# An expert's second products follow its first ones by three steps instead of two

## Chip and metric

The kernel runs on one core of a Trainium2 chip. The metric is device microseconds per execution. The engines are named as in the profile: PE (matrix products), PEld (PE's weight loads, beside the products), DVE, ACT and POOL (elementwise work), SP (issues most DMAs). Each engine takes its own instructions strictly in order, so an instruction that waits holds everything queued behind it on that engine.

## What is computed

Three layers, one behind the other, on 3072 tokens of width 384.

```python
# 1. gated linear attention, 4 x 8 heads, 768 steps, head width 48
state = f[:, :, t, :, None] * state + einsum('bhd,bhe->bhde', k[:, :, t], v[:, :, t])
y[:, :, t] = einsum('bhd,bhde->bhe', q[:, :, t], state)
# 2. eight experts, one per token, and only for tokens with x @ w_skip > 0
h = maximum(xc[mask] @ w1[e], 0.0)                    # 384 -> 1024
y[mask] = gate_w[mask, None] * (h @ w2[e])            # 1024 -> 384
out[do_compute] = xc + y
# 3. dense gated layer, 384 -> 1536 -> 384, on all tokens
xn = x / rms * rms_g
return silu(xn @ w_gate) * (xn @ w_val) @ w_out
```

## The kernel before

The attention takes the first 175 us or so. It works on 24 tiles of 128 tokens and scatters each finished token row to a slot in DRAM: tokens of expert e to the 256 slots of that expert, tokens that skip the experts to a part of their own.

Then the eight experts run, one after the other, in `expert(e)`. Values are kept as pairs of 16-bit numbers, a high and a low part, so each product is made of three. `exT` holds the expert's 256 token rows, transposed. The 1024 hidden units are cut into KF = 8 blocks of 128, and a step m works on one block:

- `up(m)`, the first products: 9 matmuls (L1041) of 256 columns into the PSUM tile `ph`, of which there are four, taken in turn by m. Then `relu`: ACT writes the high part `hh` (L1044), and DVE, which needs `hh`, writes the low part `hl` (L1045).
- `down(m)`, the second products: for each of the two halves of 128 tokens three matmuls (L1088) of 384 columns, with `hh`, `hh` and `hl` as weights, added up over all m in the PSUM tiles `ey`.

The order of the steps is written out in the loop at the end of `expert`:

```python
for m in range(KF + LAG):
    if m < KF:
        up(m)
    if m >= LAG:
        down(m - LAG)
    yield
```

The tiles `hh` and `hl` have LAG + 2 buffers. Expert 0 is a special case: the first 96 of its rows were already multiplied ahead, so its `up` has 160 columns.

Each `yield` hands over to `run`, which takes steps of work for other parts from two queues, `run(expert(e), N2)` with N2 = (1.1, 2.2): on average 1.1 steps from the first and 2.2 from the second. These steps are placed behind the newest `relu` (`tc.issue_after` on its ACT and its DVE instruction). The first queue prepares weights: load a piece of an expert's w1 or w2 into one of four buffers `st` (L357, SP) and split it into high part (L406, ACT) and low part (L407, DVE). Before expert e starts, its weights' remaining steps are taken at once (`need`); expert e + 3 is put in the queue when expert e is done. The second queue finishes tokens (`place`, `first`, `middle`): add the expert's result to the token row (L483 DVE, L484 POOL; L481 POOL for rows without an expert), the sum of squares (L488 ACT), its root (L489, L490 POOL), the normed row in two parts `xn` (L494 ACT, L495 DVE), some small copies (L510 to L513, L533, L534), and then either a scatter to the DRAM tensor `xnd` (L514 POOL) or, for the tokens of blocks 0 and 1 of the dense layer, a transposing DMA into `xnT` (L535 SP).

The dense layer starts with `pair`, blocks 0 and 1 of 512 tokens, 12 first products each (L892, `pwg` and `pwv`), then their second products (L915). Its weights are split by `prep_in` (L199 to L203 and L450 on DVE, L449 on ACT), which is queued when the experts are done; the scheduler moves some of it up beside the last experts.

The written order is not the final one. A scheduler lays out each engine's queue from its own idea of times, and moves an instruction ahead where it believes the one before it would wait.

Of the kernel before, what the change touches and what calls it, by code (L numbers as in the profile page):

```python
# [52 lines left out]
XB = 13  # L53
OTB = 3
SPLIT = 2
LAG = 2
WARM2 = 0
WN = 128
WAT = 1.0
# [26 lines left out]
def fused_kernel(ctx, tc, q, k, v, f, w_skip, w_gate, w1, w2, g_gate, g_val, g_out, rms_g, out, dbg=None):  # L86
# [956 lines left out]
    def relu(hh, hl, ph):  # L1043
        a = nc.scalar.activation(out=hh, in_=ph, func=AF.Relu)  # L1044
        b = nc.vector.scalar_tensor_tensor(out=hl, in0=ph, scalar=0.0, in1=hh, op0=ALU.max, op1=ALU.subtract)  # L1045
        pins.append((a.ins, b.ins))
# [13 lines left out]
    def expert(e):  # L1060
# [13 lines left out]
        def up(m):  # L1074
            ph = ps.tile([128, 1, CAP - c0], F32, **bank(m % 4), name="ph")
            products(e, xT, ph, (m,), c0, CAP)
            if c0:
                hs[m] = [a[:, m, :] for a in h]
            else:
                hs[m] = [ek.tile([128, CAP], F16, tag="h" + a, name="h" + a, bufs=LAG + 2) for a in "hl"]  # L1080
            relu(hs[m][0][:, c0:CAP], hs[m][1][:, c0:CAP], ph[:, 0, :])

        def down(m):
            hh, hl = hs.pop(m)
            for t in range(CAP // 128):
                sl = slice(t * 128, (t + 1) * 128)
                for j, (a, w) in enumerate(((hh, w2h), (hh, w2l), (hl, w2h))):
                    nc.tensor.matmul(py[t], lhsT=a[:, sl], rhs=w[:, m, :], start=(m == 0 and j == 0), stop=(m == KF - 1 and j == 2))  # L1088
# [7 lines that stand above are left out]
# [131 lines left out]
```

## Time and profile before

| | us |
|---|---|
| median of three runs | 765.24 |
| lowest, highest | 763.53, 768.19 |
| the profiled execution | 761.93 |
| its span, first to last instruction | 760.2 |
| PE busy in the span | 718.8 (95%) |
| DVE busy | 446.9 (59%) |
| ACT busy | 340.0 (45%) |
| POOL busy | 197.6 (26%) |

The profiled execution took 1.7 us more than its span and 3.3 us less than the median. PE's busy time counts matmuls from start to modelled end, and neighbours overlap, so it says where PE sits idle, not how fast it is while busy; the granted clock says the latter. The shares are means over stages that differ: attention to about 175 us, experts to about 336, dense layer to the end.

### The profile page before, as it was taken

How to read it: one execution, taken by the hardware profiler on the slowest of the kernel's cores; microseconds unless marked ns; L12 is line 12 of the kernel's file. 1: busy time of each engine (PE TensorE's matmuls, PEld its weight loads, DVE VectorE, ACT ScalarE, POOL GpSimd, SP SyncE). 2: the span in 40 equal slices, each digit the busy share in tenths (PEclk: the TensorE clock that was granted, in tenths of full speed). 3: DMA queues.
4: the chain of work that ended last, by engine and by line, in shares of the span. 5: the costliest groups of instructions: out<-in, count | busy, mean ns of one | idle time of the engine just before them, and what ended most of it. 6: DMA issues, size and time to landing. Idle time of an engine off the chain costs nothing.

```text
span 760.2 us, 14086 instructions
## 1 busy us (share of the span) xinstructions
PE 718.8 (95%) x5452; PEld 442.6 (58%) x5452; DVE 446.9 (59%) x955; ACT 340.0 (45%) x773; POOL 197.6 (26%) x274
## 2 busy tenths in 40 slices
PE   8999989896999879799999999999999999999995
PEld 4788878785766556454444565445454554454443
DVE  2788767885788878999997100534443454332230
ACT  5878757643767766566554111221312231222131
POOL 5222455541365556554000021000200020001002
PEclk9999999998999998899999999999999999999998
DMA  9999978746588998855453410321521150001001
GB/s 156 180 195 200 209 181 206 230 134 195 160 271 263 272 232 256 274 141 199 125 167 123 84 42 32 94 61 65 166 83 65 61 167 0 1 1 43 1 0 47
DMA packets 172890, 102.25 MB, mean 135 GB/s; under 512 B 137720, under 2 KB 151336, under 8 KB 172816
## 3 DMA queue, kind: packets, MB, share of 16 engines
q1 hardware_dynamic: 168336, 88.60, 46.4%
q0 software_dynamic: 4480, 12.67, 4.5%
q8 instruction: 45, 0.74, 0.4%
q14 instruction: 29, 0.24, 0.1%
HBM read 78.33 MB, written 16.24 MB: 124 GB/s over the span
## 4 chain that ended last, share of the span: by engine, by line
PE 73%; DMA 8%; DVE 6%; ACT 4%; POOL 4%; issue 3%; SPq 0%; POOLq 0%; ACTq 0%; DVEq 0%
PE po L915 18%; PE pwv L892 18%; PE pwg L892 18%; DMA xnd<-xn,at 4%; PE sc L666 3%; PE py L682 3%; DMA st<-in_moe_w_dram 3%; PE py L677 2%; PE ptq L648 1%; PE ptk L648 1%; DVE w2l L407 1%; PE pm L658 1%; PE lg L698 1%; PE px L703 1%; POOL xs L783 1%
## 5 line engine op out<-in xcount | busy, mean ns | idle before, releaser
L898 DVE SCALAR_TENSOR_TENSOR hf<-pwv,sg 128x512 f32<-128x512 f32 x72 | 49.6, 691 | 147.1 <-PE pwv L892 126.1
L923 POOL DMA_INDIRECT out_dram<-ot,ids x24 | 23.7, 986 | 370.9 <-ACT ot L922 366.3
L892 PE MATMUL pwg<-xnT,wgh 128*128 128x512 f16 x432 | 105.5, 379 | 0.7 <-DMA xnT<-xn 0.7
L892 PE MATMUL pwv<-xnT,wvh 128*128 128x512 f16 x432 | 105.5, 379 | 0.0
L901 ACT CAST gh<-hf 128x512 f16<-128x512 f32 x72 | 44.4, 616 | 115.2 <-DVE hf L898 115.1
L915 PE MATMUL po<-wol,gh 128*128 128x384 f16 x288 | 93.7, 326 | 0.0
L915 PE MATMUL po<-woh,gh 128*128 128x384 f16 x288 | 93.7, 326 | 0.0
L915 PE MATMUL po<-woh,gl 128*128 128x384 f16 x288 | 93.4, 326 | 0.0
L896 ACT ACTIVATE sg<-pwg 128x512 f32<-128x512 f32 x72 | 42.6, 594 | 101.1 <-PE pwg L892 101.0
L915 PEld LDWEIGHTS <-gh 128*128 128x128 f16 x576 | 56.3, 98 | 41.8
L892 PEld LDWEIGHTS <-wvh 128*128 128x128 f16 x432 | 42.3, 98 | 50.5
L902 DVE TENSOR_TENSOR gl<-hf,gh 128x512 f16<-128x512 f32 x72 | 49.9, 696 | 35.9 <-ACT gh L901 35.9
L892 PEld LDWEIGHTS <-wgh 128*128 128x128 f16 x432 | 42.2, 98 | 47.7 <-issue 1.2
L1041 PE MATMUL ph<-exT,w1h 128*128 128x256 f16 (+1 forms) x384 | 58.2, 277 | 6.9 <-DMA exT<-xs 6.9
L892 PE MATMUL pwv<-xnT,wvl 128*128 128x512 f16 x216 | 58.9, 379 | 0.0
L892 PE MATMUL pwg<-xnT,wgl 128*128 128x512 f16 x216 | 58.9, 379 | 0.0
L1041 PEld LDWEIGHTS <-w1h 128*128 128x128 f16 x432 | 40.9, 102 | 19.2 <-DMA exT<-xs 7.0
L629 POOL TENSOR_TENSOR qs<-q,ep 128x384 f32<-128x384 f32 x24 | 28.8, 1202 | 73.3 <-ACT ep L625 58.1
L1088 PE MATMUL ey<-w2h,hh 128*128 128x384 f16 x112 | 37.9, 339 | 8.1 <-ACT hh L1044 8.1
L922 ACT ACTIVATE ot<-po 128x384 f32<-128x384 f32 x24 | 11.6, 489 | 61.4 <-PE po L915 53.1
L915 PEld LDWEIGHTS <-gl 128*128 128x128 f16 x288 | 28.2, 98 | 18.6
L1088 PE MATMUL ey<-w2h,hl 128*128 128x384 f16 x112 | 31.9, 342 | 6.7 <-DVE hl L1045 5.5
(204 smaller groups left out, 1383.3 us busy)
## 6 DMA issues: line engine op xcount, KB each, us to landing
st<-in_moe_w_dram SPq DMA_DIRECT2D x32, 768.0 KB, 5.7
st<-in_moe_w_gate_dram SPq DMA_DIRECT2D x12, 768.0 KB, 4.4
st<-in_moe_w_val_dram SPq DMA_DIRECT2D x12, 768.0 KB, 4.5
st<-in_moe_w_out_dram SPq DMA_DIRECT2D x12, 768.0 KB, 4.3
f<-in_f_logit_dram SPq DMA_DIRECT2D x24, 192.0 KB, 4.6
q<-in_q_dram SPq DMA_DIRECT2D x24, 192.0 KB, 4.2
k<-in_k_dram SPq DMA_DIRECT2D x24, 192.0 KB, 4.4
v<-in_v_dram SPq DMA_DIRECT2D x24, 192.0 KB, 4.5
```

Source lines behind the costliest of these rows:

```text
L629: scaled.append(nc.gpsimd.tensor_tensor(out=qs[:, :, 0:D], in0=ins["q"], in1=ep, op=ALU.mult).ins)
L666: nc.tensor.matmul(scs[r][:, j, :], lhsT=T["k"][64 * r:64 * r + 64, j, :], rhs=T["q"][64 * r:64 * r + 64, j, :], start=True, stop=True)
L682: nc.tensor.matmul(py[64 * r:64 * r + D, j, :], lhsT=ins["v"][:, 2 * j + r, :], rhs=A[r][:, j, :], start=False, stop=(j == HP - 1), skip_g ...
L892: nc.tensor.matmul(p, lhsT=w, rhs=x, start=(j == 0), stop=(j == len(terms) - 1))
L896: nc.scalar.activation(out=sg, in_=pg, func=AF.Silu, scale=1.0 / SG)
L898: nc.vector.scalar_tensor_tensor(out=hf, in0=pv, scalar=SH / SG, in1=sg, op0=ALU.mult, op1=ALU.mult)
L901: nc.scalar.copy(out=hh, in_=hf)
L902: gated.append(nc.vector.tensor_tensor(out=hl, in0=hf, in1=hh, op=ALU.subtract).ins)
L915: nc.tensor.matmul(po[t], lhsT=a[:, sl], rhs=w, start=(m == 0 and j == 0), stop=(m == KF2 - 1 and j == 2))
L923: sc = nc.gpsimd.indirect_dma_start(out=out, out_offset=bass.IndirectOffsetOnAxis(ap=at[:, t:t + 1].bitcast(U32), axis=0), in_=ot, in_offs ...
L1041: nc.tensor.matmul(out[:, i, :], lhsT=a, rhs=r, start=(j == 0), stop=(j == len(terms) - 1))
L1088: nc.tensor.matmul(py[t], lhsT=a[:, sl], rhs=w[:, m, :], start=(m == 0 and j == 0), stop=(m == KF - 1 and j == 2))
```

## The change

LAG becomes 3. So `down(m)` is written behind `up(m + 3)` instead of behind `up(m + 2)`, the tiles `hh` and `hl` have five buffers instead of four, and the loop of an expert has 11 turns instead of 10, so that `run` hands out 12.1 and 24.2 steps per expert instead of 11 and 22. No instruction of the computation is added or removed.

```diff
 OTB = 3
 SPLIT = 2
-LAG = 2
+LAG = 3
 WARM2 = 0
```

What this does to the queues is seen at three places. On PE, the start of expert 1's second products. `ph_3719` is the first product m = 2 of expert 1 before and `ph_3745` is m = 3 after; `hh_3676` and `hh_3678` are the high part of m = 0. Before:

```order
L1041 MATMUL ph_3719<-exT_3660,w1l_3477 128x256
L1088 LDWEIGHTS hh_3676
L1088 MATMUL ey0_3664<-w2h_3556,hh_3676 128x384
L1088 LDWEIGHTS hh_3676
L1088 MATMUL ey0_3664<-w2l_3557,hh_3676 128x384
L1088 LDWEIGHTS hl_3677
L1088 MATMUL ey0_3664<-w2h_3556,hl_3677 128x384
```

and now:

```order
L1041 MATMUL ph_3745<-exT_3662,w1l_3477 128x256
L1088 LDWEIGHTS hh_3678
L1088 MATMUL ey0_3666<-w2h_3550,hh_3678 128x384
L1088 LDWEIGHTS hh_3678
L1088 MATMUL ey0_3666<-w2l_3551,hh_3678 128x384
L1088 LDWEIGHTS hl_3679
L1088 MATMUL ey0_3666<-w2h_3550,hl_3679 128x384
```

`down(0)` starts one whole `up` later, right behind the last matmul of m = 3 instead of m = 2.

On DVE, from the last low part `hl` of expert 1 to the first of expert 2. Here `w2l` is a piece of a later expert's weights, and `x` begins the finishing of expert 1's tokens. Before:

```order
L1045 SCALAR_TENSOR_TENSOR hl<-ph,hh 128x256 x2
L407 SCALAR_TENSOR_TENSOR w2l<-st_3868,w2h 128x4x192
L149 TENSOR_REDUCE big<-w2h 128x1
L407 SCALAR_TENSOR_TENSOR w2l<-st_3868,w2h 128x4x192
L407 SCALAR_TENSOR_TENSOR w2l<-st_3906,w2h 128x4x192
L1045 SCALAR_TENSOR_TENSOR hl<-ph,hh 128x256
L483 SCALAR_TENSOR_TENSOR x_3939<-ey_3664,exr 128x384
```

and now:

```order
L1045 SCALAR_TENSOR_TENSOR hl<-ph,hh 128x256
L149 TENSOR_REDUCE big<-w2h 128x1
L407 SCALAR_TENSOR_TENSOR w2l<-st_3832,w2h 128x4x192
L407 SCALAR_TENSOR_TENSOR w2l<-st_3894,w2h 128x4x192 x2
L495 SCALAR_TENSOR_TENSOR xn<-x_3803,m_3806,xn 128x384
L1045 SCALAR_TENSOR_TENSOR hl<-ph,hh 128x256
L483 SCALAR_TENSOR_TENSOR x_3939<-ey_3666,exr 128x384
```

The first `hl` of expert 2 now stands behind three pieces of `w2l` and an `xn`, where it stood behind three pieces (the first row before holds two `hl`, the last of expert 1 and the one ahead of it).

On DVE, behind the last low part of expert 7, which is the last of all. The `xn` written from `x_5329` before and from `x_5292` now is the last row tile that block 1 of the dense layer waits for. Before:

```order
L1045 SCALAR_TENSOR_TENSOR hl<-ph,hh 128x256
L483 SCALAR_TENSOR_TENSOR x_5376<-ey_5032,exr 128x384
L533 COPY ms_x<-m_5332 128x1
L199 TENSOR_SCALAR fb<-st_5754 128x768
L513 TENSOR_SCALAR at<-exr 128x1
L511 COPY xn<-exr 128x4
L495 SCALAR_TENSOR_TENSOR xn<-x_5329,m_5332,xn 128x384
```

and now:

```order
L1045 SCALAR_TENSOR_TENSOR hl<-ph,hh 128x256
L511 COPY xn<-exr 128x4
L495 SCALAR_TENSOR_TENSOR xn<-x_5292,m_5303,xn 128x384
L199 TENSOR_SCALAR fb<-st_5754 128x768
L510 SCALAR_TENSOR_TENSOR ms_x<-exr,m_5368 128x1
L495 SCALAR_TENSOR_TENSOR xn<-x_5342,m_5346,xn 128x384
```

Five rows stood between that `hl` and that `xn`; now one does.

## Rows read from the trace of the kernel before

**Rows 1.** Busy time of each engine in five stretches of the span, in us (the stretch, its length, then PE, PEld, DVE, ACT and POOL with their instruction counts, the granted TensorE clock as a share of full speed, the DMA share and GB/s). The experts run from 181.5 to about 336.

```profile
181.50:195.00 13.50, 13.48 (x116) 10.76 (x117) 7.19 (x15) 6.87 (x15) 0.00 (x0) 0.88 0.81 231
195.00:246.00 51.00, 48.66 (x365) 34.64 (x364) 42.20 (x95) 37.46 (x85) 28.35 (x35) 1.00 0.78 242
246.00:297.00 51.00, 43.25 (x299) 29.27 (x297) 41.84 (x84) 33.83 (x79) 30.13 (x37) 0.93 0.96 252
297.00:336.40 39.40, 33.93 (x214) 21.21 (x211) 38.99 (x84) 24.52 (x63) 23.80 (x30) 0.91 0.78 240
340.00:470.00 130.00, 130.00 (x674) 65.77 (x673) 75.60 (x132) 46.50 (x97) 14.43 (x15) 1.00 0.38 111
```

**Rows 2.** The chain of work that ended last, from 176 to 340 us, in order of time (its shares by line, then some of its pieces: start, length, what).

```profile
by line: DMA xnd<-xn,at 16.5%; DMA st<-in_moe_w_dram 12.0%; issue 8.4%; DVE w2l L407 6.3%; PE ph L1041 4.1%; ACT w2h L406 3.8%; DVE hl L1045 3.6%; DVE xn L495 3.3%; DVE w1l L407 3.1%; PE ey L1088 3.0%; POOL m L489 2.8%; ACT w1h L406 2.8%; P
...
192.41 0.64 PE ph L1041 x9
...
196.00 6.21 DMA st<-in_moe_w_dram
...
273.32 9.69 DMA xnd<-xn,at
...
333.64 2.71 DMA xnT<-xn
...
336.49 2.10 PE pwg L892 x9
```

**Rows 3.** PE's instructions in order of time, those in the experts' part before which PE sat idle (start, length, instruction; in brackets the idle time just before it and what ended it).

```profile
210.45 0.34 PE L1088 MATMUL ey<-w2h,hh 128*128 128x384 f16 x1 [0.68 <-ACT hh L1044]
...
251.28 0.34 PE L1088 MATMUL ey<-w2h,hh 128*128 128x384 f16 x1 [0.88 <-ACT hh L1044]
...
253.41 0.50 PE L1088 MATMUL ey<-w2h,hl 128*128 128x384 f16 x2 [1.09 <-DVE ids L534]
...
264.90 0.34 PE L1088 MATMUL ey<-w2h,hh 128*128 128x384 f16 x1 [0.97 <-ACT hh L1044]
...
279.42 0.34 PE L1088 MATMUL ey<-w2h,hh 128*128 128x384 f16 x1 [0.93 <-ACT hh L1044]
...
284.55 0.50 PE L1088 MATMUL ey<-w2h,hh 128*128 128x384 f16 x1 [3.01 <-ACT hh L1044]
...
311.89 0.34 PE L1088 MATMUL ey<-w2h,hh 128*128 128x384 f16 x1 [0.45 <-ACT hh L1044]
...
316.37 0.82 PE L1088 MATMUL ey<-w2h,hl 128*128 128x384 f16 x2 [3.34 <-DVE hl L1045]
```

**Rows 4.** Groups of instructions by line from 195 to 336 us (line, engine, operation, tiles, shapes, count | busy us, mean ns of one | idle us of the engine before them and what ended it).

```profile
L1088 PE MATMUL ey<-w2h,hh 128*128 128x384 f16 x112 | 37.9, 339 | 8.1 <-ACT hh L1044 8.1
...
L1088 PE MATMUL ey<-w2h,hl 128*128 128x384 f16 x112 | 31.9, 342 | 6.7 <-DVE hl L1045 5.5 <-DVE ids L534 1.1
...
L407 DVE SCALAR_TENSOR_TENSOR w2l<-st,w2h 128x768 f16<-128x768 f32 x26 | 28.1, 1099 | 4.5 <-ACT w2h L406 4.4
L407 DVE SCALAR_TENSOR_TENSOR w1l<-st,w1h 128x768 f16<-128x768 f32 x24 | 27.5, 1145 | 0.4 <-ACT w1h L406 0.2
...
L495 DVE SCALAR_TENSOR_TENSOR xn<-x,m,xn 128x384 f16<-128x384 f32 x26 | 18.2, 700 | 5.9 <-ACT xn L494 5.5
```

**Rows 5.** Who waited for whom from 181.5 to 336 us, DVE first, then ACT (us in total, times, longest us).

```profile
DVE xn L495 <- ACT xn L494: 5.5, 7, 2.4
DVE w2l L407 <- ACT w2h L406: 5.2, 8, 2.0
DVE at L513 <- DMA xnd<-xn,at: 3.1, 1, 3.1
DVE hl L1045 <- ACT hh L1044: 2.2, 3, 1.4
...
ACT xn L494 <- POOL m L490: 12.5, 12, 2.9
...
ACT hh L1044 <- PE ph L1041: 4.7, 5, 2.0
```

**Rows 6.** PE's instructions in order of time where nothing holds them (one step of expert 1), the first full-speed second product after each of the two long stalls, and one DVE instruction beside the POOL instruction that it overlaps.

```profile
200.37 0.49 PE L1041 MATMUL ph<-exT,w1l 128*128 128x256 f16 x3
200.70 0.33 PE L1088 MATMUL ey<-w2h,hh 128*128 128x384 f16 x1
200.86 0.33 PE L1088 MATMUL ey<-w2l,hh 128*128 128x384 f16 x1
...
290.70 0.33 PE L1088 MATMUL ey<-w2h,hh 128*128 128x384 f16 x1
...
321.33 0.33 PE L1088 MATMUL ey<-w2h,hh 128*128 128x384 f16 x1
...
251.49 1.53 DVE L495 SCALAR_TENSOR_TENSOR xn<-x,m,xn 128x384 f16<-128x384 f32 x1
...
251.68 0.92 POOL L481 TENSOR_TENSOR x<-xr 128x384 f32<-128x384 f16 x1
```

**Rows 7.** The last piece of the dense layer's first weights that DVE splits (instructions in order of time), and, from the chain of work that ended last, the last first product of its blocks 0 and 1 and the second products behind it.

```profile
382.25 1.28 DVE L450 SCALAR_TENSOR_TENSOR wvl<-fb,gsc,wvh 128x256 f16<-128x256 f32 x3
...
422.12 1.94 PE pwv L892 x9
424.06 46.80 PE po L915 x288
```

## Prediction

> **What bounds the kernel now.** I read the busy time by stretch first [rows 1]. In the dense layer PE is busy 130.00 of 130 us, so nothing is to be won there by feeding it better. The experts' part, 181.5 to 336.4, is the only one that the change touches. Up to 246 PE is busy 48.66 of 51 us at full clock. From 246 to 297 it is 43.25 of 51 at a granted clock of 0.93, and from 297 to 336.4 it is 33.93 of 39.4 at 0.91. So PE loses time in the second half, while DVE is at 38.99 of 39.4 us at the end and at 41.84 of 51 before that.
>
> Next the chain that ended last in that part [rows 2]. PE holds 4.1% and 3.0% of its 164 us, 11.6 us in all, and that is the start, 181.5 to 193. From there to 336.49 the chain runs through DMAs (the `xnd` scatter 16.5%, weight loads 12.0%), DVE, ACT and POOL, and ends with an `xn`'s transposing DMA, landing after 2.71 us. That speaks against a gain: PE's stalls are not on that chain.
>
> Then the stalls themselves [rows 3], each before a `down`, and each ended by `hh` or `hl` (an `ids` copy next to an `hl` once). Counting products from the start, the rows are expert 1 m = 6 (0.68), expert 4 m = 0 (0.88, then 1.09 in the same `down`), expert 4 m = 6 (0.97), expert 5 m = 4 (0.93) and m = 5 (3.01), and expert 7 m = 0 (0.45, then 3.34). In all PE idles 8.1 + 6.7 = 14.8 us before the second products [rows 4]. The two long stalls cost more than their length. Second products after them last 0.50 us and more instead of 0.33 [rows 3, 6], which is the lower of the two clock levels, 1.2 instead of 2.4 GHz. Full speed is back at 290.70 and 321.33 [rows 6]. That is 6.15 and 4.96 us at half rate, or 3.1 and 2.5 us lost. The stalls of 0.97 and 1.09 were not followed by this.
>
> **What the change moves, and its price.** No instruction of the computation is added, so the sum is made of stalls. A `down(m)` is covered by what PE has queued between the last matmul of `up(m)` and the first of `down(m)`. Three first products start 0.33 us apart in sum, 0.11 each, and a second product takes 0.16 [rows 6]. Counted in the two built orders:
> - m = 3 and 4: 18 first and 12 second products before, 3.9 us; now 27 and 18, 5.9 us.
> - m = 5: 3.9 us before, now 18 and 18, 4.9 us. m = 6: 10 and 12, 3.1 us; now 9 and 18, 3.9 us. m = 7: 3.1 us; now 4 and 18, 3.4 us.
> - m = 0: 18 and 6, 2.9 us; now 27 and none, 2.9 us. Before, the scheduler had stretched this for experts 4 (25 and 6, 3.7 us) and 7 (27 and 6, 3.9 us); now they have 2.9 and 3.3. So the head of an expert gains nothing and at two experts loses.
>
> Step by step, if the helpers (ACT, DVE, POOL) deliver when they do now:
> - Middle stalls shown: 0.68 goes, 0.97 shrinks by 0.9, 0.93 goes, 3.01 shrinks by 1.0. Sum 3.5.
> - The small ones: 14.8 less the 11.35 of rows 3 leaves 3.45. Most lie where the cover grows by 0.3 to 2 us; I take three quarters, 2.6. With the line above 6.1 us saved.
> - Heads: at expert 4 the `hl` product now comes 0.33 us behind the first one, with 2.9 of cover; before it had 3.7 and, between the two waits, 0.87 of other products. Lost 1.3. At expert 7, 3.9 less 3.3 is 0.6 lost. Sum 2.0, rounded up.
> - Net on PE: 4.1 us, from 6.1 - 2.0.
>
> What of it reaches the end? DVE's only idle time that ends on `hh` is 2.2 us in three waits, and ACT's on `ph` 4.7 us in five, while ACT waits 12.5 us for POOL's `m`, and DVE 5.5 for `xn`, 5.2 for `w2h` and 3.1 for a scatter [rows 5]. Those are latencies among the helpers and stay as they are. So between 0 (the helpers' chain sets the end) and 4.1 us (PE does) I take the middle, 2.0 us, since the chain speaks for the first and PE's busy share to 246 for the second.
>
> The rest goes together. Buffers: a fifth `hh` and `hl` add no wait. PSUM: `up(m + 4)` needs the tile of m, and `down(m)` stands ahead of it, so the four tiles just suffice. The 11th turn hands out 1.1 and 2.2 more steps per expert, all behind the last `relu`. In the built order, DVE's queue between the last `hl` of an expert and the first of the next grows by one split piece at two boundaries (1.1 each [rows 4]), one `xn` at one (0.7 [rows 4]), about 1.2 at another and 1.0 at the last, some 5.1 in sum, none at two. Who waits for that is the next expert's `down(0)`. As DVE's total is unchanged, I count nothing for it in the forecast and price it below. SP keeps its sequence of weight loads, with a few neighbours swapped; a load still waits for one of four `st`. At the end, the last `xn` for `xnT` has five rows fewer ahead of it, two of them of an `xn`'s size (some 1.3 us by its mean of 0.70), but PE now has one `down` more queued ahead of that point, 6 times 0.16, 1.0 us. Neither counts. The dense layer can start earlier without running dry: its last weights are split at 382.25 + 1.28 = 383.5 and first used by the 21st of 24 `up`s, four of them (each two of 1.94) before 424.06, at 408.5 [rows 7]. That is 25 us of room.
>
> The profiled execution took 761.93, 3.3 below the median of 765.24. The sum gives 759.9 for a profiled one, and **763** for a median.
>
> **Rivals.**
> *Helpers set the end, no gain: 765.2.* Behind it stands the chain without PE [rows 2], and DVE full from 297 on [rows 1]. Against it is that DVE idles 9 us of the 51 before that. One `xn` lasted 1.53 us beside a POOL instruction of 0.92 [rows 6], where its mean is 0.70 [rows 4], so the two engines hold each other up at times.
> The Trainium skill, SBUF — State Buffer, section "SBUF: two separate sides", says that a DVE instruction with two SBUF inputs and a POOL instruction share one pair of ports under an exclusive lock. The row agrees; by that rule the helpers' time can't be squeezed by letting them overlap better, and this rival's time is what comes out.
>
> *PE is followed by the helpers: 756.1.* The 6.1 us of middle and small stalls go and the heads don't get worse, since a PE without stalls hands `ph` over earlier. The stall of 3.01 shrinks to 2.0 and the clock holds, 3.1 us more. Together 9.2 us. For it: PE's share to 246 and the 3.1 and 2.5 us paid for the clock. Against it: ACT waits little for `ph`.
> The Trainium skill, TensorE: Matmul & The Clock Gate, section "Loop structure matters more than you think", says that a loop that waits between its matmuls runs cold and a dense one stays at full clock. By that the change would earn the clock back besides the stalls, which is this rival; the rows behind the two long stalls agree, those behind the short ones show no loss.
>
> *The heads get worse: 775.* The mechanism is the first `hl` of an expert behind a denser DVE queue: 5.1 us of growth over five boundaries, plus 2.0 of lost cover, plus the clock falling at two more experts (2.8 each, the mean of 3.1 and 2.5), 12.7 us. With all of the middle savings it is 6.6, without them 12.7; I take 10. It decides once the first `hl` comes more than 3.3 us after its `up`; at expert 7 it came 8.4 after (3.9 + 0.45 + four products + 3.34).
>
> *The change does little that the scheduler had not done:* at experts 4 and 7 `up(3)` already stood ahead of much of `down(0)`. That gives the time of the first rival and is in its chance.
>
> **How the numbers follow.** The three runs spread over 4.7 us, 0.6%, so about 1%, 7.65 us, is what a measurement can tell from no change. Chances: forecast 0.45, no gain 0.28, PE followed 0.14, heads worse 0.13. The first two lie within 1%; of the third 0.12 lies beyond 757.6 and of the fourth 0.10 beyond 772.9. So faster 0.12, same 0.78, slower 0.10. The range for 8 in 10 takes in the first two with their bounds and some of each of the others: 754 to 774.
>
> **What would show it.** In the trace after, the `down`s of m = 3 to 6 should wait for almost nothing, and PE's idle time before second products should fall from 14.8 to some 10 us, most of it at m = 0 of experts 4 to 7. The chain between 193 and the first `pwg` should hold next to no PE, and that `pwg` should start 0 to 4 us earlier than 336.49. DVE should still be full at the end. I am wrong if the experts' part shortens by over 7 us, or if waits of over 3 us stand at the head of several experts with slow products behind them.

## The result and the profile after

The kernel became slower. Its median is 773.05 us (771.61 to 774.39) beside 765.83 for the kernel before on the same chip, a ratio of 1.0096 (95% interval 1.0069 to 1.0123); a second comparison gave 1.0122 (1.0102 to 1.0142). The forecast of 763 us was wrong in sign. The profiled execution took 773.05 us, with a span of 771.3.

The experts start 4.7 us later in this trace (186.2 instead of 181.5; the first experiment shows this to be chance). So the busy time by stretch, which answers to [rows 1], is taken with all borders 4.7 us later (same columns; the last stretch ends with the last second product):

```profile
186.20:199.70 13.50, 13.50 (x115) 10.79 (x116) 7.96 (x16) 7.83 (x16) 0.00 (x0) 0.87 0.88 256
199.70:250.70 51.00, 45.77 (x333) 32.87 (x332) 37.04 (x85) 33.83 (x78) 28.51 (x31) 0.93 0.79 221
250.70:301.70 51.00, 43.55 (x314) 30.58 (x311) 41.90 (x88) 35.12 (x80) 32.98 (x40) 0.97 0.91 251
301.70:346.00 44.30, 34.34 (x222) 21.93 (x223) 41.87 (x88) 26.18 (x65) 27.44 (x32) 0.92 0.78 222
```

In the first 51 us of the experts DVE had been busy 42.20 us and PE 48.66 at full clock [rows 1]; now it is 37.04 and 45.77 at a clock of 0.93, and the last second product comes 44.30 us into the last stretch where it came 36.5 us into it (at 333.5; the 39.4 us of [rows 1] reach on to a wait of the dense layer). DVE's total over the whole span hasn't changed, 447.0 us and 446.9 before. So DVE has no more to do; it waits more. Who it waited for (186 to 346 us, same columns as [rows 5]):

```profile
DVE at L513 <- DMA xnd<-xn,at: 6.0, 5, 2.3
DVE at L513 <- issue: 5.6, 1, 5.6
DVE xn L511 <- issue: 5.0, 1, 5.0
DVE xn L511 <- DMA xnd<-xn,at: 2.7, 1, 2.7
DVE hl L1045 <- ACT hh L1044: 2.1, 2, 1.5
...
DVE xn L511 <- DMA xnT<-xn: 0.9, 1, 0.9
```

And before, at the same copies, besides the 3.1 us in [rows 5] (181.5 to 336 us):

```profile
DVE xn L511 <- DMA xnT<-xn: 1.6, 2, 1.3
DVE xn L511 <- DMA xnd<-xn,at: 1.0, 2, 0.7
```

L511 and L513 are small copies of some 0.15 us: they put a row tile's tail into `xn` and its list of rows into `at`, just ahead of its scatter to `xnd`. Before them DVE idled 20.2 us, where it had idled 5.7. ACT's `xn`, which goes into the same buffers, waited 11.2 us for scatters, where it had waited 6.6. "issue" means that the profile names no releaser; what it was is seen further down.

PE's second products with more than 0.9 us of idle time before them, in order of time, which answers to [rows 3], and two of those behind the second stall:

```profile
232.64 0.34 PE L1088 MATMUL ey<-w2h,hh 128*128 128x384 f16 x1 [1.89 <-ACT hh L1044]
236.29 0.50 PE L1088 MATMUL ey<-w2h,hl 128*128 128x384 f16 x1 [3.15 <-DVE hl L1045]
236.58 0.53 PE L1088 MATMUL ey<-w2h,hh 128*128 128x384 f16 x1
236.90 0.53 PE L1088 MATMUL ey<-w2l,hh 128*128 128x384 f16 x1
256.81 0.34 PE L1088 MATMUL ey<-w2h,hl 128*128 128x384 f16 x1 [2.48 <-DVE hl L1045]
274.72 0.34 PE L1088 MATMUL ey<-w2h,hl 128*128 128x384 f16 x1 [1.37 <-DVE hl L1045]
277.06 0.34 PE L1088 MATMUL ey<-w2h,hl 128*128 128x384 f16 x1 [1.02 <-DVE hl L1045]
284.90 0.34 PE L1088 MATMUL ey<-w2h,hl 128*128 128x384 f16 x1 [1.79 <-DVE hl L1045]
302.31 0.34 PE L1088 MATMUL ey<-w2h,hl 128*128 128x384 f16 x1 [0.92 <-DVE hl L1045]
312.64 0.34 PE L1088 MATMUL ey<-w2h,hl 128*128 128x384 f16 x1 [0.99 <-DVE hl L1045]
315.73 0.50 PE L1088 MATMUL ey<-w2h,hl 128*128 128x384 f16 x2 [1.51 <-DVE hl L1045]
320.01 0.50 PE L1088 MATMUL ey<-w2h,hl 128*128 128x384 f16 x2 [1.17 <-DVE ids L534]
328.62 0.82 PE L1088 MATMUL ey<-w2h,hl 128*128 128x384 f16 x2 [5.50 <-DVE hl L1045]
```

Counting products, these are expert 2 m = 6 (twice), expert 3 m = 6, expert 4 m = 5 and 6, expert 5 m = 0, expert 6 m = 0, 5, 6 and 7, and expert 7 m = 0. Nearly all end on `hl`, DVE's part; before, most ended on ACT's `hh`.

**The place itself.** POOL, DVE, ACT and PE around the stall of 3.15, in order of time (start, length, instruction, idle time before it and what ended it):

```profile
219.92 1.07 POOL L514 DMA_INDIRECT xnd<-xn,at  x1 [5.09 <-DVE xn L495]
...
226.56 0.15 DVE L513 TENSOR_SCALAR at<-exr 128x1 int32<-128x1 f32 x1 [2.30 <-DMA xnd<-xn,at]
...
227.64 0.62 DVE L495 SCALAR_TENSOR_TENSOR xn<-x,m,xn 128x384 f16<-128x384 f32 x1
...
228.54 1.87 POOL L514 DMA_INDIRECT xnd<-xn,at  x1 [3.62 <-DVE xn L495]
...
235.61 0.15 DVE L513 TENSOR_SCALAR at<-xr 128x1 int32<-128x1 f32 x1 [5.62 <-issue]
235.63 0.61 ACT L494 ACTIVATE xn<-x,m 128x384 f16<-128x384 f32 x1 [2.55 <-DMA xnd<-xn,at]
235.82 0.42 DVE L1045 SCALAR_TENSOR_TENSOR hl<-ph,hh 128x256 f16<-128x256 f32 x1
236.15 0.61 DVE L495 SCALAR_TENSOR_TENSOR xn<-x,m,xn 128x384 f16<-128x384 f32 x1
...
237.05 1.18 POOL L514 DMA_INDIRECT xnd<-xn,at  x1 [3.83 <-DVE xn L495]
```

`xn` and `at` have two buffers each. Call the four row tiles A, B, C and D; in DVE's built order of the changed kernel the last three are `xn_3963`, `xn_4000` and `xn_4087`:

```
L513 TENSOR_SCALAR at_4030<-exr_3664 128x1
L511 COPY xn_4000<-exr_3664 128x4
...
L495 SCALAR_TENSOR_TENSOR xn_3963<-x2_3939,m2_3943,xn_3963 128x384
L1045 SCALAR_TENSOR_TENSOR hl_4048<-ph_4037,hh_4047 128x256
...
L1045 SCALAR_TENSOR_TENSOR hl_4077<-ph_4066,hh_4076 128x256
...
L513 TENSOR_SCALAR at_4092<-xr_4035 128x1
L511 COPY xn_4087<-xr_4035 128x4
...
L1045 SCALAR_TENSOR_TENSOR hl_4108<-ph_4097,hh_4107 128x256
L495 SCALAR_TENSOR_TENSOR xn_4000<-x2_3992,m2_3996,xn_4000 128x384
L495 SCALAR_TENSOR_TENSOR xn_4087<-x2_4059,m2_4062,xn_4087 128x384
```

A's scatter is issued at 219.92 and its buffers come free at 226.56. C's copies, which write into them, wait for that on DVE, and B's `xn` (227.64) stands behind C's copies. So B's scatter starts only at 228.54. D's copies need B's buffers. ACT's `xn` beside them, released at 235.63 by the scatter, shows what ended DVE's wait of 5.62: B's scatter had landed, 5.2 us after its issue ended at 230.41. (The copies need D's raw row too, but POOL had read that at 230.76, in L481.) Behind D's copies stand C's `xn` (236.15) and an `hl` that PE wants (235.82). Each tile's copies hold up the tile before it, whose late scatter holds up the next copies: a convoy. Its own part can be sized here: without the wait of 2.30 B's `xn` would have run some 2.3 us earlier (ACT had its high part ready at 224.78), so about 2.3 of the 5.62 us were fed on from one wait to the next, and 3.3 are the scatter itself. A wait of 4.97 us follows at the copies of a later tile (256.13). That one is hardly fed, since the copies ahead of it had waited only 0.30 us (246.76): it is the time of one scatter, whose issue ended at 251.02, met too early.

In the built orders all 22 such copies stand ahead of their own tile's `xn`, in both kernels, since they need only the raw row. Ahead of the `xn` of the tile before stand 5 of them in the kernel before and 10 in the changed one.

The longest stall of PE, 5.50 us at the start of expert 7, is of another kind. DVE waits for nothing between the last `hl` of expert 6 (319.55) and the next (328.15): three pieces of `w2l`, two `xn` and pieces of the dense layer's weights stand between them, 8.6 us where it was 7.1 before (308.84 to 315.90) with a stall of 3.34.

The clock adds to it. From 236.2 to 241 the granted clock is 0.52 and second products come 0.32 us apart (236.58 and 236.90) where [rows 6] has 0.16; from 256.7 to 262 it is 0.68, from 328.5 to 334 it is 0.59. Out of 4.8, 5.3 and 5.5 us that is 2.3, 1.7 and 2.2 us lost, 6.2 in all, where the kernel before lost 3.1 and 2.5. Counted in the same way, the second traces of the two kernels (first experiment) have 7.2 and 2.7, so the clock adds 0.6 us in the one pair of traces and 4.5 in the other.

What it comes to: from the first `ph` of expert 0 that waits for its rows (181.5 before, 186.2 after) to the dense layer's second products (423.9 and 435.1; the chain has them at 424.06 [rows 7] and 435.24) it is 242.4 us before and 248.9 after, 6.5 more. The two long waits stand on the chain of work that ended last (start, length, what):

```profile
230.00 5.61 issue
...
251.16 4.97 issue
```

### The profile page after: what moved, and what is told of

Read it like the earlier page. It is cut to its first block, busy times and chain, and to the rows that moved or that the text cites. A ratio compares the mean times of both kernels' runs of the same rounds, so it can differ in the third digit from the quotient of the medians.

```text
span 771.3 us, 14085 instructions
## 1 busy us (share of the span) xinstructions
PE 719.6 (93%) x5452; PEld 444.7 (58%) x5452; DVE 447.0 (58%) x955; ACT 340.7 (44%) x773; POOL 203.7 (26%) x274
## 4 chain that ended last, share of the span: by engine, by line
PE 57%; DVE 5%; DMA 3%; issue 3%; POOL 2%; ACT 1%; ACTq 0%; POOLq 0%; DVEq 0%
PE po L915 18%; PE pwv L892 18%; PE pwg L892 18%; DMA xnd<-xn,at 3%; PE ey L1088 2%; DVE w2l L407 1%; PE ph L1041 1%; DVE xn L495 1%; DVE hl L1045 1%; DMA xnT<-xn 1%; POOL m L490 0%; DVE w1l L407 0%; POOL xnd L514 0%; POOL x L484 0%; DVE fb L201 0%
## 5 line engine op out<-in xcount | busy, mean ns | idle before, releaser
L902 DVE TENSOR_TENSOR gl<-hf,gh 128x512 f16<-128x512 f32 x72 | 49.9, 693 | 36.5 <-ACT gh L901 34.9
L1041 PE MATMUL ph<-exT,w1h 128*128 128x256 f16 (+1 forms) x384 | 55.1, 279 | 7.0 <-DMA exT<-xs 7.0
L1088 PE MATMUL ey<-w2h,hl 128*128 128x384 f16 x112 | 37.1, 344 | 20.7 <-DVE hl L1045 19.4
L514 POOL DMA_INDIRECT xnd<-xn,at x22 | 31.2, 1417 | 35.8 <-DVE xn L495 33.1
L915 PEld LDWEIGHTS <-gl 128*128 128x128 f16 x288 | 28.2, 98 | 18.6
```

The source lines that it names most:

```text
L514: sc = nc.gpsimd.indirect_dma_start(out=xnd, out_offset=bass.IndirectOffsetOnAxis(ap=at.bitcast(U32), axis=0), in_=xn, in_offset=None, bou ...
L902: gated.append(nc.vector.tensor_tensor(out=hl, in0=hf, in1=hh, op=ALU.subtract).ins)
L915: nc.tensor.matmul(po[t], lhsT=a[:, sl], rhs=w, start=(m == 0 and j == 0), stop=(m == KF2 - 1 and j == 2))
L1041: nc.tensor.matmul(out[:, i, :], lhsT=a, rhs=r, start=(j == 0), stop=(j == len(terms) - 1))
```

## The experiments

The table has, for each kernel, the ratio to the kernel before (runs beside it on the same chip), and from its trace the length of the **stage** just defined, **DVE's idle time at row tiles** (the brackets before L483, L495, L510, L511, L513, L533 and L534, added up from 8 us into the stage to the last second product of the experts), and **PE's idle time** in the same span. These lengths are of one execution for each trace: that of the last row took 759.59 us, the shortest of its twelve (median 762.82), so its stage lies low.

| kernel | ratio, 95% interval | stage | DVE at row tiles | PE idle |
|---|---|---|---|---|
| before, two traces | 0.9997 (0.9978 to 1.0016) | 242.4, 242.4 | 11.2, 9.6 | 14.7, 15.8 |
| after, two traces | 1.0122 (1.0102 to 1.0142) | 248.9, 249.2 | 23.0, 25.8 | 22.5, 22.1 |
| LAG 3, 10 turns | 1.0020 (1.0004 to 1.0036) | 242.5 | 11.6 | 17.9 |
| LAG 2, 11 turns | 0.9974 (0.9958 to 0.9990) | 239.0 | 14.5 | 14.8 |
| LAG 3, 3 buffers | 1.0001 (0.9983 to 1.0019) | 241.9 | 9.2 | 17.7 |
| LAG 2, 3 buffers | 0.9982 (0.9957 to 1.0007) | 238.9 | 9.1 | 12.8 |
| LAG 3, rows' steps in 10 turns | 1.0107 (1.0075 to 1.0140) | 249.7 | 23.5 | 23.1 |
| LAG 3, weights' steps in 10 turns | 1.0063 (1.0032 to 1.0094) | 245.1 | 8.9 | 16.1 |
| LAG 3, copies on POOL | 1.0101 (1.0075 to 1.0127) | 246.1 | 18.6 | 19.9 |
| LAG 2, 11 turns, 3 buffers | 0.9998 (0.9980 to 1.0015) | 238.8 | 6.9 | 15.3 |
| LAG 3, copies behind `xn` | 0.9965 (0.9942 to 0.9988) | 239.6 | 11.5 | 10.3 |
| LAG 2, copies behind `xn` | 0.9947 (0.9923 to 0.9971) | 237.8 | 8.9 | 13.9 |
| LAG 2, 1 buffer | 1.0772 (1.0731 to 1.0812) | 301.3 | 34.0 | 50.1 |
| LAG 3, 10 turns, 3 buffers | 0.9988 (0.9968 to 1.0008) | 237.0 | 6.6 | 12.3 |

**The two kernels again.** Nothing is edited.

> The kernel before, unchanged, for a second trace of it. In the first trace the experts' first product starts at 181.5 us and in the changed kernel's at 186.2, though nothing of the attention's order on PE differs. If that is chance, this trace's start lies anywhere between 181 and 186; if it belongs to the change, it lies within 1 us of 181.5. The time should be 766, the ratio 1.000 within 0.003.

> The changed kernel (LAG = 3), unchanged, for a second trace and a second comparison. Ratio 1.0096 again, within 0.003. If the later start of the experts belongs to the change, the first product starts at 186 us again; if it was chance, somewhat earlier, and then the stretch from there to the first product of the dense layer must still be some 5 us longer than the 155.0 us of before.

The experts started at 184.3 us in both traces. So the later start in the first trace after was chance, and 6.5 to 6.8 us in the stage are the change's. The two long copies' waits came back on the spot (5.69 and 4.96 us).

**The extra turn, with and without the distance.**

```diff
             if m >= LAG:
                 down(m - LAG)
-            yield
+            if m < KF + 2:
+                yield
```

> LAG = 3, but the loop of an expert hands out steps of side work in 10 turns as before, none in the 11th. Theory A (the 11th turn's steps, all placed behind the last relu of an expert, make DVE's queue longer ahead of the next expert's first low part, and PE waits there): the time goes back to 766 or below, 763 if the longer distance also saves the middle stalls. Theory B (the order of PE's own queue is what costs: a second product that waits now stands ahead of more, and the scheduler no longer mixes products at the head): 773 stays.

With LAG = 3 and ten turns the loss is all but gone, 765.18 beside 763.92 (0.2% are left). That speaks for theory A. The opposite, LAG = 2 with an empty eleventh turn (one more `yield` behind the loop), refutes it as stated:

> The distance of two steps as before, but an expert's loop has an empty 11th turn that hands out 1.1 and 2.2 more steps. Theory A: 772 to 774, the changed kernel's time without its distance. Theory B: 766.

It took 761.50 beside 763.92, faster. More steps per expert, and the longer DVE queue that they make, cost nothing by themselves. Only both together did, so the cause had to lie in how things came to stand. Its trace has 11.2 us of waits at the copies too, one of them 4.9 us, and yet it is faster than the kernel before: the sum of these waits alone doesn't set the time, it matters what stands behind them.

**A third buffer.** The traces suggested the row tiles.

```diff
-        xn = nk.tile([128, ROW], F32, tag="xn", name="xn")
+        xn = nk.tile([128, ROW], F32, tag="xn", name="xn", bufs=3)
...
-        at = nk.tile([128, 1], I32, tag="at", name="at")
+        at = nk.tile([128, 1], I32, tag="at", name="at", bufs=3)
```

> LAG = 3 with three buffers instead of two for the finished row tile xn and its list of rows at. Theory C: the extra turn makes three row tiles follow each other closely, the third waits on DVE (5.6 and 5.0 us at its small copies, 20 us in all against 6 before) until the scatter of the first has landed, and the low parts hl queue behind it. Then DVE's waits for xnd fall below 6 us, the 3.2 and 2.5 us stalls at m = 6 of experts 2 and 3 go, and the time falls by 5 to 9 us, to 764 to 768. Rival D (DVE's queue simply holds more work ahead of an expert's first low part; the buffer waits take place where DVE has nothing urgent): 770 or more stays.

> The distance of two as before, with the third buffer for xn and at. Theory C: DVE waited only 4 to 6 us for these buffers there, so the gain is 0 to 2 us (762 to 764). Rival D: 764. Should it fall as far as the other kernel does, the buffers are a cost of both kernels and not what the change brought.

LAG = 3 took 765.04 beside 764.30, LAG = 2 took 763.53: the buffer is worth 7 to 9 us to the one and at most 3 to the other. The time is the one that theory C named. Of the stalls that it named, that of 3.15 us is gone and that of 2.48 is down to 2.0 in two pieces; expert 7 still starts with one of 5.61, which therefore is not what the change costs on balance. Of the 20 us at the copies these are left in the former (DVE's waits, 181.5 to 346 us):

```profile
DVE at L513 <- DMA exr<-xs: 1.6, 1, 1.6
DVE xn L511 <- DMA xnT<-xn: 1.6, 2, 1.0
DVE xn L511 <- DMA xnd<-xn,at: 1.5, 1, 1.5
```

The order of the other instructions moves with the buffer, so it is not the wait alone that was taken away.

**Which of the two queues.** LAG = 3, eleven turns, where the eleventh hands out steps of one queue only (`yield m < KF + 2`, and in `run` a test that leaves the other queue out).

> LAG = 3, where the 11th turn hands out its 1.1 steps of the weights' queue but none of the rows' queue. Theory C: the rows' steps are what collides, so 764 to 767. Rival D (the weights' pieces of 1.1 us each fill DVE's queue at the boundary): 771 or more.

> LAG = 3, where the 11th turn hands out its 2.2 steps of the rows' queue but none of the weights' queue. Theory C: 771 to 774 stays. Rival D: 764 to 767.

Both are misses for theory C as I had put it, and the first came out as rival D said: without the rows' extra steps the loss stayed whole (773.66), with the rows' and without the weights' it shrank (770.12 beside 764.30), to a time that neither had named. By the waits at the copies (19.2 us in the first, 6.2 in the second) it is still the row tiles that collide, but it is not the number of their steps that brings it about. That rival D's pieces alone do it is unlikely, since the third buffer left all of them in place and took the loss away; how much they add is not shown. The second kernel is still 0.6% slower, and not by this mechanism; its dense layer starts late (PE waits 2.48 us for ACT at its first products). That was not followed up.

**The copies on POOL.** L511 and L513 become `nc.gpsimd` instead of `nc.vector`.

> LAG = 3 with two buffers as in the changed kernel, but the two small copies of a row tile that waited on DVE for the last scatter but one (into the tail of xn, and the list at) are made on POOL, which issues the scatter anyway. Theory C (DVE, held by these copies with low parts hl queued behind, is what the change costs): 764 to 768, DVE's waits for xnd gone, though ACT may still wait for a buffer xn. Rival E (the third buffer helped because it makes the finishing of rows as a whole quicker, whichever engine waits): 770 or more.

767.60 beside 760.50: a miss. DVE no longer waits at copies, but at `xn`, which waits for ACT, which waits for POOL's `m` that the copies now delay (181.5 to 346 us):

```profile
DVE xn L495 <- ACT xn L494: 12.8, 12, 4.5
...
ACT xn L494 <- POOL m L490: 15.7, 13, 4.8
```

The ratio, 1.0101, is what rival E said (771.7 by a before of 764). But as the edit moved the wait and didn't remove it, it can't tell the two theories apart.

**relu first.** Both instructions of `relu` inside `tc.high_priority(HOFF)`.

> LAG = 3 with two buffers, where the scheduler is told to put the two instructions of relu (high and low part) ahead of other work that is ready. Theory F (the distance gave PE more cover, but the scheduler used it to lay more side work ahead of each low part, so that the stalls at m = 4 to 6 stayed): these stalls go, 760 to 766. Rival G (the low parts are late because ACT and DVE have too much to do in total or wait, in whatever order): 770 to 775.

> The distance of two with relu's instructions ahead of other work that is ready. Theory F: the short cover suffices too, 758 to 764. Rival G: 762 to 768.

The scheduler laid out the same queues as without it, so these were two more runs of the kernels after and before: 1.0119 (1.0094 to 1.0145) and 0.9995 (0.9971 to 1.0019). Theories F and G were not told apart here.

**Both single gains together.**

> The distance of two, 11 turns and the third buffer for xn and at: the two single changes that lay lowest (761.5 and 763.5), together. With 11 turns DVE waited 11 us for the buffers (three of these waits of 2.4 to 4.9 us). If what theory C says holds there too, 758 to 761; if those waits lay where nothing urgent was queued behind, 761 to 763.

759.74 beside 760.50, no difference, though its stage was the second shortest of those with LAG = 2. The gains don't add up.

**The copies behind their own `xn`.** The buffers stay at two, and no work moves to another engine.

```diff
-        nc.vector.scalar_tensor_tensor(out=xp[:, 1, :], ...
+        low = nc.vector.scalar_tensor_tensor(out=xp[:, 1, :], ...
...
-        nc.vector.tensor_copy(out=xn[:, DM:], in_=mt)
+        with tc.issue_after(low): nc.vector.tensor_copy(out=xn[:, DM:], in_=mt)
...
-        nc.vector.tensor_scalar(out=at, ...
+        with tc.issue_after(low): nc.vector.tensor_scalar(out=at, ...
```

> LAG = 3 with two buffers; the two small copies of a row tile are placed behind the same tile's low part xn on DVE, so that they can no longer overtake it and wait there for the last scatter but one. Theory C2 (a convoy: the copies of one tile stand ahead of the xn of the tile before it, whose scatter so goes out late, and the next tile's copies wait for that scatter): DVE's idle time at row tiles falls from 23 to 26 us to under 14, and the time to 762 to 766. Rival E (with only two buffers the rows' finishing is as slow in any order, and the wait only moves to xn behind ACT): DVE's idle time at row tiles stays over 18 us, and the time at 768 or more by a before of 764.

> The distance of two with the copies placed behind xn in the same way. Theory C2: there was hardly a convoy, so -2 to +1 us. Rival E: the same, 0. It tells what the placing itself costs or brings.

LAG = 3 took 762.00 beside 763.61, faster than before instead of 1.2% slower, and DVE's idle time at row tiles fell to 11.5. This is theory C2's result, with the reserve that here too other instructions moved with the edit. LAG = 2 took 759.72, the lowest ratio of this study, 0.5% below the kernel before. That is more than the -2 to +1 us expected, and DVE's idle time at row tiles fell by only 0.7 to 2.3 us, so where it comes from is not shown; the placing may bring something besides the waits. At LAG = 3 it brings 1.3 to 1.6%, though, 0.8 to 1.0% more than here, and that difference is about what the change had cost. Who DVE waited for with LAG = 3 (181.5 to 328 us): no copy is left among them.

```profile
DVE eal L1045 <- ACT eah L1044: 9.0, 3, 6.5
DVE xn L495 <- ACT xn L494: 8.9, 8, 2.6
DVE hl L1045 <- ACT hh L1044: 2.2, 2, 1.5
DVE ids L534 <- DMA xr<-xs: 2.1, 2, 1.2
```

And its second products with over 0.5 us of idle time before them:

```profile
253.36 0.34 PE L1088 MATMUL ey<-w2h,hh 128*128 128x384 f16 x1 [2.29 <-ACT hh L1044]
254.37 0.50 PE L1088 MATMUL ey<-w2h,hl 128*128 128x384 f16 x1 [0.51 <-DVE hl L1045]
288.38 0.34 PE L1088 MATMUL ey<-w2h,hl 128*128 128x384 f16 x1 [0.53 <-DVE hl L1045]
291.04 0.34 PE L1088 MATMUL ey<-w2h,hl 128*128 128x384 f16 x1 [0.69 <-DVE hl L1045]
302.83 0.34 PE L1088 MATMUL ey<-w2h,hh 128*128 128x384 f16 x1 [1.73 <-ACT hh L1044]
308.01 0.34 PE L1088 MATMUL ey<-w2h,hh 128*128 128x384 f16 x1 [0.76 <-ACT hh L1044]
311.37 0.34 PE L1088 MATMUL ey<-w2h,hl 128*128 128x384 f16 x1 [2.86 <-DVE hl L1045]
```

These are m = 0 of expert 4 (twice), 6 and 7 (twice), m = 1 and 7 of expert 6. From m = 2 to 6 none of this length is left.

**One buffer, the distance of two.**

> The distance of two with one buffer for xn and at instead of two. If waits for scatters on DVE are what costs, whatever the distance, DVE's idle time at row tiles rises from 10 to over 25 us, and the time by 5 to 15 us. If a distance of two bears such waits without loss, it stays within 2 us, and the buffers can't explain the changed kernel by themselves.

It took 823.63 us, 60 more; the mechanism as expected, the size four times the upper end. The waits at the copies made 30.2 us. The longest stall of PE is something else:

```profile
DVE xn L511 <- DMA xnd<-xn,at: 20.1, 9, 4.7
```

```profile
359.92 0.48 PE L1088 MATMUL ey<-w2h,hh 128*128 128x384 f16 x1 [20.96 <-DVE ids L534]
```

PE needs the PSUM tile `ey` of an earlier expert, which DVE reads (L483) only at 359.26, behind pieces of the dense layer's weights; DVE is busy for 19.02 of the 20.96 us. So with too few buffers a distance of two loses as well, but part of the 60 us comes from an order that the edit changed, and what the waits alone make of it is not shown.

**The distance alone.**

> The distance of three with the two repairs together, 10 turns and three buffers. Its counterpart is the distance of two with three buffers, 0.998 of before. If the distance alone is worth what the prediction's step on the middle stalls said (6.1 us saved, 2.0 lost at the heads), the ratio is 0.993 here; if the low parts simply come later by as much as the cover grew, 0.998 to 1.002.

The ratio is 0.9988 (0.9968 to 1.0008), its counterpart's 0.9982 (0.9957 to 1.0007), and with the copies behind `xn` it is 0.9965 for three steps and 0.9947 for two, with overlapping intervals. So where the waits at the copies are short, three steps instead of two bring nothing that can be measured. A gain of the 4.1 us that the prediction had on PE, 0.54%, lies outside these intervals; one of 2.0 us, 0.26%, is at the edge of the first pair's.

## Why the prediction was wrong

**The step that failed** is the one on what reaches the end: it read the helpers' waits in [rows 5], the 3.1 us at a scatter among them, as latencies that "stay as they are", and let DVE's queue at the boundaries count nothing "as DVE's total is unchanged". The total did stay (446.9 and 447.0). The waits didn't: those at the copies went from 5.7 to 20.2 us. A reordering doesn't change what DVE has to do, but it does change what stands behind an instruction that waits for a buffer, and how late the release is that the next one waits for. [rows 5] had the line, and the chain [rows 2] had `xnd` as its first item with 16.5%; I took it for a transfer on the way, and didn't look for the buffers behind it.

**The middle stalls**, 6.1 us saved: not in the changed kernel, where 13.6 us of the stalls shown stand at m = 5 to 7. With the copies behind `xn` most of them did go. PE's idle time is 10.3 us there, and 7 of the 9.4 us shown stand at m = 0. The text had said "from 14.8 to some 10 us, most of it at m = 0 of experts 4 to 7". But that compares two edits at once. Against LAG = 2 with the same repair, PE's idle time at m = 1 to 7 falls from 6.4 to 3.3 us there and from 6.7 to 4.1 with 10 turns and three buffers, and with 11 turns and three buffers it rises from 6.7 to 10.3. So the cover works the way that the text said, at half the size, where DVE isn't held; 6.1 was too much there too.

**The heads**, 2.0 us lost: m = 0 costs 1.79 + 0.92 + 5.50 = 8.2 us over experts 5 to 7, where [rows 3] has 5.8 at m = 0 of experts 4 and 7, so 2.4 more; in the second traces it is 11.0 beside 7.5, so 3.5 more. That the size is near is luck: at expert 4, where 1.3 us were to be lost, PE has no stall there at all, and experts 5 and 6, for which nothing had been said, have 1.79 and 0.92.

**What reaches the end of a saving on PE**: the first rival's mechanism, helpers set the end, is what one pair of repaired kernels shows. With LAG = 3 and the copies behind `xn` the last second product comes 142.8 us into the stage, against 147.6 with LAG = 2. Yet the stage isn't shorter (239.6 and 237.8). The dense layer starts earlier and then runs dry twice, since ACT's `sg`, which frees the PSUM tile, is queued behind row tiles and weight parts. These wait for a scatter (1.50 us at 329.19, ahead of the first), and for DVE, POOL's `x` and POOL's `m` (2.04, 1.53 and twice 0.66 us from 347 to 354.5, ahead of the second):

```profile
330.33 1.46 PE L892 MATMUL pwg<-xnT,wgh 128*128 128x512 f16 x6 [1.83 <-ACT sg L896]
...
356.85 1.44 PE L892 MATMUL pwg<-xnT,wgh 128*128 128x512 f16 x3 [3.04 <-ACT sg L896]
```

```profile
328.00:340.00 12.00, 10.17 (x48) 4.51 (x47) 12.00 (x23) 8.12 (x21) 5.01 (x7) 1.00 0.61 176
```

Together these are 4.9 us, where LAG = 2 with the same edit waits 0.54 us (336.63), and 4.8 us is all that the last second product came earlier. In the second fence (a stretch with the columns of [rows 1]) DVE is busy 12.00 of 12 us. The claim that the dense layer "can start earlier without running dry" was wrong: it looked at the last piece of the weights alone, and not at what else stands in ACT's and DVE's queues at the start.

**The rival "heads get worse", 775**, lay near the measured time for another reason. Its mechanism was 5.1 us more work in DVE's queue; LAG = 2 with eleven turns has that growth in steps and is faster. The mechanism is there at expert 7 (8.6 us of queue instead of 7.1, a stall of 5.50 instead of 3.34), but it stays with the third buffer, where the loss goes. Of the clock it priced 5.6 us more; it was 0.6 more in the first traces and 4.5 in the second. The measured time lies inside the range of 754 to 774 only because the upper end had been set for this rival; that is luck too.

**The clock.** After the stalls of 3.15 and 2.48 us the granted clock fell, and the second and third rows of the first fence have 0.93 and 0.97. With the copies behind `xn` and no stall in that time it is at full clock (LAG = 3, the columns of [rows 1]):

```profile
195.00:246.00 51.00, 50.76 (x389) 37.52 (x388) 43.00 (x92) 38.68 (x89) 28.17 (x35) 1.00 0.81 239
```

The Trainium skill, TensorE: Matmul & The Clock Gate, section "Loop structure matters more than you think", says that a loop with long waits between its matmuls runs cold and one whose matmuls follow back to back stays warm; these rows agree. What it made of the time in the prediction's second rival, 756.1, needed a loop that the change had made dense, and the change didn't.

**What stays open.** Why the built order with LAG = 3 and the weights' eleventh turn lets the row tiles collide, and with ten turns doesn't. Counting copies ahead of the `xn` before them doesn't settle it: 10 in the changed kernel with 20 us of waits, but 9 with ten turns and 7 us. With three buffers it is even 16, and 5 us. It probably takes tiles that follow each other closely besides, and what spaces them was not isolated. Nor was it measured over the whole kernel how much of the 14 us of added waits the convoy feeds and how much are single scatters that the copies meet too early; of the two longest, 10.6 us in sum, it fed some 2.6. And as every edit here moves other instructions too, it is not shown that the waits at the copies are all of the cost.

## To carry to other kernels

When an edit moves instructions, look for the ones that write into a buffer that a DMA still reads, above all small ones with early inputs, which a scheduler likes to place far ahead: on an in-order engine they hold everything behind them until the transfer has landed, and if the tile whose transfer they wait for is itself behind them, the waits feed each other. A busy time that doesn't change says nothing about waits. Before costing a longer software pipeline, ask whether its helpers deliver late for lack of cover or because they are held up; more cover helps only with the first.

## What was not expected of the hardware

A scatter of one row tile (128 x 388 words of 4 bytes, 194 KB as the profile counts) freed its buffer 5.2 us after POOL had finished issuing it (230.41 to 235.6), beside a load of 768 KB and one of 388 KB issued at 229.48 and 229.95; the one before took 5.6 us (220.99 to 226.56). The Trainium skill, DMA: Bandwidth & Descriptors, section "Anatomy of one DMA — SWDGE (gpsimd) path", gives a fit of 2.0 us plus the bytes at 436 GB/s for a transfer of this path, 2.5 us for this size as an estimate from that page. Under load the trace doesn't agree: it shows twice that, measured from the end of the issue to the release. In the kernel before, the scatters issued from 195 to 336 us took 3.9 to 9.7 us from the start of their issue to landing, at the median 4.9, with a DMA share of 0.78 to 0.96 [rows 1]; the two issued between 344 and 356 us, with a share of 0.49, took 2.7 us, near the page's estimate. That points to the load beside it as the reason, which no run here isolated.
